# Closing an attention and FFN kernel by whole PSUM banks, with a new instruction order

## Chip, cores and metric

One NeuronCore of a Trainium2 chip runs the whole program. The metric is the device time of one execution in microseconds (us). Engines are named as in the profile: PE (TensorE), ACT (ScalarE), DVE (VectorE), POOL (GpSimd), SP (the DMA queue).

## What is computed

```python
xn  = layernorm(x)                       # x: 1 x 2048 x 640
q   = (xn @ wq) -> 32 heads of 20        # wq: 640 x 640
k, v = xn @ wk, xn @ wv                  # one key/value head of 20 for all heads
p   = softmax(q k^T / sqrt(20))          # 32 x 2048 x 2048
A   = concat(p v) @ wo                   # wo: 640 x 640
B   = silu(xn @ w1) @ w2                 # w1: 640 x 1728, w2: 1728 x 640
out = x + A + B                          # bfloat16
```

## The kernel before

**Tiles.** The 2048 query rows are cut into four chunks of 512 (`qc`), the heads into eight groups of four. A chunk and a head group form one of 32 groups (`g`), and each has 16 key tiles of 128. One score tile is 128 keys by 512 queries of one head: 2048 of them in all. With a head dimension of 20 padded to 32, the scores of up to four heads run at the same time in four row strips of the array (a burst, `s_mm`, L1168), and the product with the values runs as four column strips, one per head (a value step, `pv_mms`, L1295).

**Two ways to exponentiate.** ACT takes runs of one, two or three neighbouring PSUM banks with one exponential (L1258). DVE takes single tiles: it writes a 16-bit integer whose bits read as a bfloat16 power of two (`p1`, L1503), and adds two shifted copies of it (`SHIFT`), by integer additions over four tiles at once, so that three value steps together give the exponential. Four such tiles are a batch. The shifted copies are made on POOL (L1542) or DVE (L1547); each kind has two buffers (`NW`). In `dve_advance` copy 2 always goes to POOL (`POOL_J`), and copy 1 as the order's token says.

**The rest of PE's work.** Q projections, the FFN's first product with a tanh on ACT, and the FFN's second product joined with the output projection (`out_job`, two halves of 320 columns per 128 rows) are cut into pieces between the scores. All of them use `col_mm` (L537), four column strips per step. A finished group is copied out of PSUM (L1344), its sums are inverted, spread by small DMAs, multiplied on POOL (L950) and packed by DMAs into `oT`.

**The end.** For the last chunk the FFN's second product is made early (`y_job`: eight jobs of 320 columns, 14 contraction steps each; for row tiles 2 and 3 with the first three of the projection's 128-row steps, `YC = (0, 0, 3, 3)`) and gathered with half weight and the residual in `yx` (L1009). The last two groups are not packed: their sums are taken by PE against a selector `sel4` (L1089), inverted (L1092), spread by PE against an identity (L1107), and multiplied (L1116). Selector and identity are rebuilt late in the run on POOL (`make_sel`, from L1627) in a slot of `qT`. Then `fin_job` lays the chunk's 2560 output columns out as five banks of 512: `finA` does the projection steps that are left and the group before the last, `finB` the last group, and each bank is evicted with the addition of `yx` on DVE (L1057) and stored (L1074).

**Order.** `build` plans every engine's instruction order from estimated costs. From a planned 36 us on it instead follows written lists: `ORDER` has one three-character token for each PE step (S or s: scores for ACT, with the number of tiles; D, E, F, G: a score tile for DVE; a, d: value steps for ACT's and DVE's tiles; n, m: first and further steps of another job), and `OTHERS` has one letter for each instruction of ACT, DVE and POOL. Where the lists end, the planner goes on by its rules. `emit` then turns the order into instructions with semaphores; PE runs strictly in that order.

Of the kernel before, what the change touches and what calls it, by code (L numbers as in the profile page):

```python
# [14 lines left out]
P = 128  # L15
D = 640
# [65 lines left out]
POOL_J = (2,)  # L82
# [4 lines left out]
YC = (0, 0, 3, 3)  # L87
# [5 lines left out]
FIN_ACT = ()  # L93
FIN_ORDER = (1, 3, 0, 2, 4)
REST = 6
OUT_ACT = (1, 3)
T_SUM = 225.0
T_SPREAD = 230.0
AHEAD = 1
# [12 lines left out]
def rule(n):  # L112
# [4 lines left out]
    "D32D13S14a97nq6m00m00D25S20Dd2m00m00S23nh5aa7S20D66m00D32D03S14m00m00m00S20S12Dd6ab7nh4m00m00m00m00S20D33D05nh6m00m00m00m00nh2S20D23Dd4m00m00m00m00ac7"  # L117
    "S20S13D45nh6m00m00m00m00S30D34ad7ae7af7d03d13d33S24D26d23S20E37D82d43d63d53S24D16a03S20D37D82d93d73dc3S34E27a13D10S11D32d83df3nh7m00S24E20Dd6m00m00m00"
    "S21D00a23da3di3S34D20db3S21Dc7a33nh0m00m00S24E36D27m00m00nh1m00m00m00m00S34D12a43de3dd3a53dg3S20E37dh3S24Dd2D26a63nh7m00S20D02m00S14Dc5D56m00m00a73S20"
    "E32s24a83nq6m00m00m00m00S20D22E37dk3dj3S24a06d06S30d36d26a16S24D93D27d66d56S20D02d96d16d46S23D95a26nh7m00S20D32m00S23D25d86m00dc6m00S20D02S15db6nh3d76"  # L120
    "m00m00m00m00S20E34De7a36a46a56D02S24da6df6S20D33dd6E17S24nh2m00m00S20De3m00D07S24m00de6dh6S20D33De7a66dg6a76S24D12a86nh3m00S20D37m00D02S24a96m00S20Da7"
    "m00d02d32a02E14D05S26d22d42S20D33nq4m00m00S25D17m00m00S20Da3a12d62S25D07a22d52S20D34d12d92S25E13D87a32d82S20D24dc2da2S25D13Dc7a42nh4m00S20E33m00S25D17"
    "m00D23S20a52db2S25Dc3D57m00a62df2de2S20D33d72a72S25Dc7nh3m00m00m00m00S20D24a82dh2S26D55nh4m00m00D30D21S13m00m00S35nh3m00m00m00m00a92S20E34s25dd2dg2a07"
    "d07d17S20Da4D33d37S25D02a17d27d67S20Da4d47S25D12D03a27d57S20D34nh2m00m00m00m00S23E15D86s20a37d97d87d77dc7D13S24Dc2a47D26S20da7nh3m00S24D52a57E36D20S11"
    "m00m00m00S24E32a67db7S20Dd6df7de7S24D02nh3m00m00m00m00S20D26Dd2s24a77dh7dd7dg7S20D63a87nq6m00S24D32m00S20D93m00m00S24D02a97d03d33S20D66a03d23S24D32D07"
    "d43S20D96a13d63S24E32nh7m00D06D20S11m00m00m00S34E32a23a33d53d93S20Dd2d73D07S24D36dc3d83nh2S20E27m00Dc6S14D25m00m00m00S20D16S17nh4m00m00m00m00db3S20D35"
    "de3a43d13S35De2a53S20D04a63nh2m00m00m00S34D37a73da3a83dd3S10E11m00S24De6D37a93nh0m00S16S11m00m00S24Da2F06S17m00aa3d01d31S24E12d21d11d61S26D03d41d51S24"
    "D10Da2a01d91S26D33nh0m00D04D15S12m00m00m00S26E33a11a21d81S24D82dc1S26D20db1dd1df1S22D14S15a31nh0m00m00m00m00de1S22D34s25Dd7a41d71da1nq4m00S22D00m00D27"
# [12 lines left out]
    "S20D15E27de2dd2S23D86a82a92D15S20no7m00S23D36m00m00m00m00aa2S20S25m00m00m00d04d14d34d24D20S11S12D93m00a04d64d54D00S11S15D36d94m00m00d84S22S10E21m00m00"
    "m00m00d44S25Dc1m00m00m00a14S22D20d74S25D11Dc7a24a34S22E30nh1m00m00m00m00S25D10s22D27a44a54da4dc4db4S20Dc5D56df4dd4S22E37de4nh5m00S20Dc6a64D27S12E33m00"
    "m00m00S20D36a74S22D17dg4dh4nh6m00S20D85a84D22D13S17m00m00m00S30S15nh7m00m00m00m00a94d03S30D36d33d23d63d53d93S24D27d83d13S20D82a03a13S24D16D27a23a33S20"
    "E32d43d73nh6S24Dd7m00m00m00m00S20D02s24D27a43a53dc3da3df3S20E36Dc2db3dg3S24D17nh6m00m00D20S11E32m00m00S24Dc7a63a73dd3S20D22de3S24D16a83nh7m00S20E32m00"
    "D86D14S15a93m00m00dh3S30D26nh5m00m00m00m00S23D87s20D32a06d06d36d26d66S33D17a16nh2m00m00m00m00d56S20s33D27a26d96d86d16d46D30D81S12d76nh7m00D13S24D20m00"
    "m00m00E31Dc2S13s24a36a46dc6S20D23da6df6db6S24D12Dc7a56S20E33dd6nh2m00S24D17a66m00m00m00S20D23E37nh4m00m00m00m00a76S20S12Dd5de6nh3m00m00m00m00S20D04S17"
    "nq2m00m00m00m00S24S10D31a86a96dg6dh6S22S24F21D87nq0m00m00m00m00S21D13a06d06S24D37d16d36S20E22D93a16d26S24D07d46d66S20D22D93a26d56S24E37d76d96a36S30D23"
    "d86S24D07dc6db6nq3m00m00S20D32m00m00S24Dc7a46a56da6S20D22dd6S24D13Dc7a66df6de6S20E32D23dg6S24a76D12s20E37Fc3dh6S24D12a86D27S20G33s24a96d02S20Da7d32d62"
    "D03S24D16a02d22S20D37no3m00m00m00S24D86d52d92S20D27m00m00m00m00d82S24S26m00m00m00m00m00m00d12S20D14D85a12m00m00m00m00S26E34m00a22S20D15a32a42S23D27E36"
    "d42d72dc2S20Dc5a52S23D27D36da2db2no5m00S20m00m00S23De6m00m00m00m00S20E17m00m00m00S23D36m00m00m00m00S20D07m00m00m00m00S23Da6a62a72a82S20D15D07a92df2S23"  # L150
    "D36de2dd2S20E15D87dg2S23D26dh2no5m00m00m00S20D17m00m00m00S32m00m00m00m00S20D96D67m00m00m00m00m00m00S32D46m00m00a07d07d17S20D36d37d27S22Dc4D55a17a27d67"
    "S20E36d47d57S22Dc4a37S25D20E31a47d87d77S22D14nq0m00S25D21m00m00m00S23Dc2a57d97S25E30D21dc7da7S22D14db7no0m00S25E31m00m00S23Dc2m00a67a77a87S21S25m00m00"
    "m00m00m00m00m00m00S21D23D34m00m00m00a97de7S25E13dd7S21Da4m00m00m00S25D03aa7d04d34d24S30D33a04S25D17d64d54d14nq3d44S30D87m00m00m00m00S25a14S20D17Dc2a24"
    "a34d94d84S25D23E37dc4db4S20D12d74no3m00S25D27m00m00S20Dc2m00m00m00a44m00S35D32m00m00m00m00m00da4S20D12m00m00S25D37m00m00m00m00a54S20E27D92a64a74S25D03"
    "a84dd4S30D27de4S25D83a94df4dh4dg4S20D37D22no3m00m00m00m00S24D16m00m00m00m00S20E37m00m00m00S34D92m00m00m00S20D07m00m00m00m00a02S34D27d02d12d32d22S20Dc3"
    "D57a12a22a32d42S24E33D26d62d52S20Dc7a42S23E35no6m00a52S20D17m00m00m00m00d92S33D37m00m00m00d72d82S20D27m00m00Dc3S14D25m00m00da2S20D17m00m00dc2S23E35db2"
    "S20Dc7m00m00m00m00a62S23D25D37a72a82S20E16de2dd2S33Db7a92aa2no6m00S20D17m00m00S32D05m00m00m00m00d07S20D25m00d17d37d27S22S14D95m00m00m00m00m00m00m00m00"
    "m00S30D03m00a07d67d47S23D25d97d57S20Dc2D56a17d87S24E33dc7d77S20Dc2a27a37S23D25E36nh2a47m00S20D15m00S23D26a57da7m00db7S25Dc0D51m00nh3m00m00m00m00S24D30"
    "S16a67nh1m00m00m00m00S32D25dd7df7a77de7S25D80a87dh7S11D32S13D24a97nh0m00dg7S25D11D82m00m00m00S23E37s25a01a11d01d11d21S22D24D30d31d41S26E15a21d61S22Da4"
# [259 lines left out]
def build(nc, A_x, A_wq, A_wk, A_wv, A_wo, B_x, B_w1, B_w2, out, stack):  # L419
# [584 lines left out]
    def y_job(qc, i, hf):  # L1004
# [8 lines left out]
        job.consumers = [op]  # L1013
        return job

    oT_op = {}
    fin_made = {}
    fin_asked = set()

# [1373 lines left out]
```

## Time and profile before

| | |
|---|---|
| runs | 681.31, 680.39, 681.21 us; median 681.21 |
| profiled execution | 681.22 us; its span, first to last instruction, 679.4 us |
| granted TensorE clock, mean | 0.995 |
| DVE's score tiles / shifts on DVE / shifts on POOL | 712 / 118 / 238 |
| exponentials of one, two, three banks | 56 / 520 / 80 |

The profile has one row for each group of instructions of one source line, engine and operation: how often, the busy time, the mean of one, and the idle time ahead of them. Busy shares are averages over the whole span; the windows cut it into stretches. In the last of 40 equal slices PE is 80% busy, DVE 30%, ACT 20% and POOL not at all.

### The profile page before, as it was taken

The numbers are of one execution on the slowest core, as the hardware profiler recorded it, in microseconds if no ns is written. First come the engines' busy times: TensorE is split into PE (matmuls) and PEld (weight loads), VectorE is DVE, ScalarE is ACT, GpSimd is POOL, SyncE is SP. The second block draws the span as 40 slices with busy tenths as digits, with TensorE's granted clock in tenths as the row PEclk, the third lists the DMA queues.
The fourth block names the chain that finished last, engine by engine and source line by source line (L and its number), as shares of the span: only waits on it lengthen the run. The fifth ranks groups of instructions, "written<-read, shape, count | busy, mean of one in ns | idle before, by whom it ended". The sixth has DMA issues, their size and how long they took to land.

```text
span 679.4 us, 22817 instructions
## 1 busy us (share of the span) xinstructions
PE 666.0 (98%) x9898; PEld 240.8 (35%) x9901; DVE 632.2 (93%) x1102; ACT 654.4 (96%) x728; POOL 514.1 (76%) x314
## 2 busy tenths in 40 slices
PE   8999999999999999999999999999999999999998
PEld 5433323332322333333333333333332333333345
DVE  7899999999998999899999999999999899999943
ACT  6999999999998999999999999999999899999992
POOL 6648787878886887876888787788888857777760
PEclk9999999999998999999999999999999899999999
DMA  8652220222221223231212222312222202233201
GB/s 224 184 180 18 32 24 14 27 26 22 34 32 24 32 30 42 29 57 25 23 27 35 36 26 34 40 31 50 21 19 35 25 20 33 31 49 43 23 7 41
DMA packets 34243, 29.00 MB, mean 43 GB/s; under 512 B 15486, under 2 KB 29662, under 8 KB 34142
## 3 DMA queue, kind: packets, MB, share of 16 engines
q1 hardware_dynamic: 33854, 27.20, 25.9%
q8 instruction: 78, 1.28, 0.8%
q10 hardware_dynamic: 288, 0.33, 0.1%
q14 instruction: 23, 0.19, 0.1%
HBM read 11.09 MB, written 2.62 MB: 20 GB/s over the span
## 4 chain that ended last, share of the span: by engine, by line
PE 63%; ACT 20%; DVE 13%; POOL 3%; issue 1%; DMA 0%; POOLq 0%; ACTq 0%
PE psall L1295 21%; PE psall L1168 20%; PE psall L537 20%; ACT sbt L1258 18%; DVE sbt L1503 7%; POOL sbt L1542 3%; ACT sbt L863 1%; DVE sbt L1547 1%; DVE sbt L866 1%; DVE sbt L653 1%; DVE sbt L697 0%; DVE sbt L655 0%; PE psall L711 0%; DVE sbt L783 0%; DVE sbt L1344 0%
## 5 line engine op out<-in xcount | busy, mean ns | idle before, releaser
L1258 ACT ACTIVATE sbt<-psall 128x1024 bf16<-128x1024 f32 (+2 forms) x656 | 624.4, 1067 | 7.1 <-PE psall L1168 5.7
L1542 POOL TENSOR_SCALAR sbt<-sbt 128x2048 int16<-128x2048 int16 x238 | 451.5, 1897 | 112.3 <-PE psall L1295 40.9
L1503 DVE TENSOR_SCALAR sbt<-psall 128x512 int16<-128x512 f32 x712 | 454.6, 682 | 20.3 <-PE psall L1168 15.2
L1295 PE MATMUL psall<-sbt 128*32 128x512 bf16 x3472 | 273.6, 386 | 2.1 <-DVE sbt L1547 0.8
L1168 PE MATMUL psall<-sbt 32*128 32x512 bf16 x2048 | 255.8, 386 | 4.4 <-ACT sbt L1258 1.0
L537 PE MATMUL psall<-sbt 128*32 128x320 bf16 (+3 forms) x3900 | 218.9, 332 | 0.4 <-DVE sbt L1503 0.2
L1168 PEld LDWEIGHTS psall<-sbt 32*128 32x128 bf16 x2048 | 69.3, 91 | 225.6 <-ACT sbt L1258 125.6
L537 PEld LDWEIGHTS psall<-sbt 128*32 128x32 bf16 (+1 forms) x3900 | 84.2, 96 | 86.8 <-issue 46.6
L1295 PEld LDWEIGHTS psall<-sbt 128*32 128x32 bf16 x3472 | 72.8, 95 | 109.2 <-issue 70.6
L1547 DVE TENSOR_SCALAR sbt<-sbt 128x2048 int16<-128x2048 int16 x118 | 80.8, 710 | 0.6 <-PE psall L1295 0.5
L950 POOL TENSOR_TENSOR sbt<-sbt 128x512 bf16<-128x512 f32 x30 | 38.5, 1284 | 20.2 <-DVE sbt L1547 16.8
L866 DVE SCALAR_TENSOR_TENSOR sbt<-sbt,psall 128x512 bf16<-128x512 bf16 x52 | 35.1, 677 | 0.1
L863 ACT ACTIVATE sbt<-psall 128x512 bf16<-128x512 f32 x52 | 32.1, 619 | 0.0
L1344 DVE COPY sbt<-psall 128x512 f32<-128x512 f32 x31 | 21.1, 681 | 0.4 <-PE psall L1295 0.3
L783 DVE TENSOR_SCALAR sbt<-psall 128x512 bf16<-128x512 f32 x20 | 13.6, 678 | 0.1
L1009 DVE SCALAR_TENSOR_TENSOR sbt<-psall,sbt 128x320 f32<-128x320 f32 x8 | 3.9, 486 | 10.2 <-PE psall L537 10.2
L662 POOL TENSOR_TENSOR sbt<-sbt 128x2 f32<-128x2 f32 x8 | 5.7, 708 | 8.5 <-DVE sbt L660 8.2
L993 DVE SCALAR_TENSOR_TENSOR sbt<-psall,sbt 128x320 bf16<-128x320 f32 x24 | 11.6, 485 | 0.2 <-PE psall L537 0.2
L675 POOL TENSOR_SCALAR sbt<-sbt 128x640 bf16<-128x640 bf16 x12 | 10.4, 874 | 1.5 <-DVE sbt L667 1.5
L653 DVE BATCH_NORM_STATS2 sbt<-sbt 128x6 f32<-128x320 bf16 x14 | 6.6, 472 | 1.9 <-DMA sbt<-in_A_x_dram 1.9
L685 PE MATMUL psall<-sbt 128*128 128x128 bf16 x80 | 6.9, 220 | 1.5 <-DVE sbt L678 1.5
L1824 PE MATMUL psall<-sbt 128*32 128x256 bf16 x144 | 6.5, 338 | 1.2 <-DVE sbt L577 1.2
(63 smaller groups left out, 98.8 us busy)
## 6 DMA issues: line engine op xcount, KB each, us to landing
sbt<-sbt SPq DMA_DIRECT2D x120, 64.0 KB, 3.8
sbt<-in_A_x_dram SPq DMA_DIRECT2D x28, 160.0 KB, 4.1
sbt<-sbt SPq DMA_DIRECT2D x213, 20.0 KB
out_dram<-sbt SPq DMA_DIRECT2D x14, 160.0 KB, 2.1
sbt<-in_B_w_dram SPq DMA_DIRECT2D x1, 2160.0 KB, 13.9
sbt<-in_B_w_dram SPq DMA_DIRECT2D x1, 2080.0 KB, 8.4
sbt<-sbt SPq DMA_DIRECT2D x75, 8.0 KB
sbt<-in_A_wq_dram SPq DMA_DIRECT2D x1, 800.0 KB, 5.8
```

What stands on the lines that cost most here:

```text
L537: ins = pe.matmul(ps[j * SLOT:(j + 1) * SLOT, b * BANK + off:b * BANK + off + n], w[:, j * SLOT:(j + 1) * SLOT], x, start=start, stop=stop ...
L783: op = Op("dve", lambda v: v.tensor_scalar_mul(q_st[:, st, :], bk(job.bank), QSCALE), t_dve(512), DVE_END, pre=[job.ready], writes=[res("q ...
L863: t = Op("act", lambda a: a.activation(t_buf[0:rows, ts, :], bk(job.bank, 0, QW, rows=rows), AF.Tanh, scale=0.5), t_act(512), ACT_END, pre ...
L866: u = Op("dve", lambda v: v.scalar_tensor_tensor(out=hT[par][0:rows, fk, :], in0=t_buf[0:rows, ts, :], scalar=1.0, in1=bk(job.bank, 0, QW, ...
L950: nm = pool(lambda e: e.tensor_tensor(oU[:, us, :], U_sb[:, us, :], Rrep, ALU.mult), 1356.0, POOL_END, pre=[uc] + lc + pack_op.get(divmod( ...
L1168: return pe.matmul(bk(b), kT_rep[i * SLOT:(i + 1) * SLOT, kt * P:(kt + 1) * P], qT[i * SLOT:(i + 1) * SLOT, g % NQ, :], start=True, stop=T ...
L1258: return a.activation(Ebuf[:, es * QW:es * QW + w], ps[:, buf[0] * BANK:buf[0] * BANK + w], AF.Exp, scale=ESCALE)
L1295: ins = pe.matmul(ps[i * SLOT:(i + 1) * SLOT, ub * BANK:ub * BANK + QW], lhsT, rhs, start=(first and k < HG), stop=(last and k >= len(lst) ...
L1344: return v.tensor_copy(U_sb[:, us, :], bk(ub))
L1503: p1 = Op("dve", lambda v: v.tensor_scalar(z16[:, i * QW:(i + 1) * QW], bk(job.bank), ZBIAS, 0.0, ALU.add, ALU.max), t_dve(QW) + 2.0, DVE_ ...
L1542: op = pool(lambda v, t=t, j=j, zin=zin: v.tensor_scalar(t.bitcast(I16), zin, float(SHIFT[j]), 1.0, ALU.add, ALU.mult), POOL_SHIFT, POOL_E ...
L1547: op = dve(lambda v, t=t, j=j, zin=zin: v.tensor_scalar_add(t.bitcast(I16), zin, float(SHIFT[j])), t_dve(N, 4), prio=SPRIO - 0.01 * j, **args)
```

## The change

- `y_job` is made per bank: five jobs of 512 columns with 14 steps, none of the projection (`YC` all zero). A bank that spans two row tiles is filled by two matmul groups per step. The sum is gathered in SBUF (`yxf`).
- A new `w_job` per bank adds the projection's first three steps (`WC = 3`) into the same SBUF sum with one more DVE operation. `y` and `w` jobs are both named in `ORDER`.
- `fin_job` is left with the projection's fourth step and the group before the last (one piece of two steps per bank); the first such piece is named in `ORDER`, too. The closing steps run in the bank order 1, 0, 2, 3, 4.
- Bank 0 is evicted by ACT into `U_sb` and added on POOL; the other four stay on DVE.
- The fp32 identity keeps an SBUF tile of its own; the selector is a strided view of it. `make_sel` and `make_two` are gone.
- A new token `J` puts both shifted copies on DVE; the packing DMAs have an earlier rank.
- `ORDER` and `OTHERS` are new from beginning to end and reach the last value step.

Counted in the lists (those before, then after): score bursts for ACT of one, two, three tiles 56/496/69, then 88/504/62; score tiles for DVE 705, then 716; value steps 831, then 863; shifts on DVE 116, then 110; shifts on POOL 234, then 250; bursts of scores, which hold ACT's and DVE's tiles together, 601, then 605.

```diff
-POOL_J = (2,)
-YC = (0, 0, 3, 3)
+YC = (0, 0, 0, 0, 0)
+WC = 3
-FIN_ACT = ()
-FIN_ORDER = (1, 3, 0, 2, 4)
+FIN_ACT = (0,)
+FIN_ORDER = (0, 1, 2, 3, 4)
+FIN_B = (1, 0, 2, 3, 4)
...
-    ident_f = s_t[-1][-1][:, 0:2 * P].bitcast(F32)
+    ident_f = sb([P, P], F32)
-    sel4 = qT[:, 2, 0:2 * HG].bitcast(F32)
-    ident_e = qT[:, 2, QW - 2 * P:QW].bitcast(F32)
...
+    def bank_mms(b, lhs, rhs, pre, reads, rows=tuple(range(HG))):
+        op = Op("pe", None, sum(t_mc(d1 - d0) for _, d0, d1, _ in segs(b)), pre=pre, reads=reads, mode="p")
+        def f(pe, bank):
+            sg = segs(b)
+            for i, d0, d1, off in sg:
+                ins = col_mm(pe, bank, d1 - d0, lhs(i), rhs(i, d0, d1), op.ends[0] and off == 0, op.ends[1] and i == sg[-1][0], off)
+            return ins
...
+    def y_job(b):
+        job = bank_job(f"y{b}", ffn_bank(b) + o_bank(b, range(YC[b])))
+        op = Op("dve", lambda v: v.scalar_tensor_tensor(out=yxf[:, b * BANK:(b + 1) * BANK], in0=bk(job.bank), scalar=0.5,
+                                                        in1=xresf[:, b * BANK:(b + 1) * BANK], op0=ALU.mult, op1=ALU.add),
...
+    def w_job(b):
+        job = bank_job(f"w{b}", o_bank(b, range(YC[b], WC)))
+        op = Op("dve", lambda v: v.scalar_tensor_tensor(out=yxf[:, b * BANK:(b + 1) * BANK], in0=bk(job.bank), scalar=0.5,
+                                                        in1=yxf[:, b * BANK:(b + 1) * BANK], op0=ALU.mult, op1=ALU.add),
...
     def fin_job(b):
+        mms += o_bank(b, range(WC, DC - 1))
+        mms.append(bank_mms(b, lambda i: oT[:, 1 - qc % 2, 1, i * P:(i + 1) * P], lambda i, d0, d1: wo_end[:, 0, d0:d1],
+                            d_wo_end, [res("oT", "end", 1, 0)]))
...
+        if b in FIN_ACT:
+            half = U_sb[:, us, :]
+            op = Op("act", lambda a: a.activation(half, bk(job.bank), AF.Copy, scale=0.5), t_act(BANK), ACT_END, pre=args["pre"], writes=[res("U", us)], prio=0.3, job=job)
+            fin_ev[b] = pool(lambda g: g.tensor_tensor(dst, half, yb, ALU.add), 1356.0, POOL_END, pre=[op], reads=[res("U", us), res("yx", b)],
+                             writes=args["writes"], prio=0.3, on_commit=args["on_commit"])
...
-                return pe.matmul(bk(b, t * HG, (t + 1) * HG), U_sb[:, us, t * P:(t + 1) * P], sel4, start=True, stop=True)
+                return pe.matmul(bk(b, t * HG, (t + 1) * HG), U_sb[:, us, t * P:(t + 1) * P], ident_f[:, DH:P:SLOT], start=True, stop=True)
...
-            if j in POOL_J or st.get("pool", pool_load() < ru.pj):
+            if j > st.get("pool", 0 if pool_load() < ru.pj else 1):
...
-    "d94d84ny2m00m00S25E37m00S20Dc3m00da4d74dc4S35D33m00m00m00m00a54S10E21m00a64S35D33m00m00m00m00db4S20D13m00m00m00S25D87a74a84S30E23a94df4S35")
+    "S16a84d94d74d84a94S30J35aa4dc4da4db4S35S13dd4de4ny0m00m00m00m00S35D21m00m00m00m00S21S13D94m00m00m00m00S34D07m00a01a11a21S22D37a31d01S34D90a41d31d11d41"
+    "S22D07D30d51d21d61S34E27a51S22D00d71ns7m00m00m00S34D30a61a71S22E27np0m00m00m00S24S26d91d81nw2m00a81da1S33dc1m00a91db1dd1de1nf6m00aa1")
```

More of the change, by code (lines that the diff above doesn't have):

```diff
@@ L1002, in build @@
     y_op = {}
-    def y_job(qc, i, hf):
-        e0, e1 = hf * HALF, (hf + 1) * HALF
-        mms = ffn_mms(qc, i, e0, e1, True, not YC[i]) + o_mms(qc, i, e0, e1, False, True, range(YC[i]))
-        job = pe_job(f"y{qc}_{i}_{hf}", mms, (14 + YC[i]) * 140, dyn=True)
-        short(job, qc)
-        op = Op("dve", lambda v: v.scalar_tensor_tensor(out=yx[:, i, e0:e1], in0=bk(job.bank, 0, HALF), scalar=0.5,
-                                                        in1=xres[:, i, e0:e1], op0=ALU.mult, op1=ALU.add),
-                t_dve(HALF), DVE_END, pre=[job.ready, xres_op[(qc, i)]] + [norm_op[n] for n in range(NT)] + [out_done[(qc - 1, t)] for t in range(QTP)], reads=[res("xres", i)], writes=[res("yx", i, hf)], prio=0.3, job=job)
-        y_op[(i, hf)] = op
[L1013 to L1018, printed above, removed]
     def segs(b):
@@ new lines, in bank_job, with xr_of @@
+    def bank_job(name, mms):
+        job = Job(name, 1100)
+        for k, op in enumerate(mms):
+            op.job, op.name, op.first, op.last = job, name, k == 0, k == len(mms) - 1
+            op.ends = (k == 0, k == len(mms) - 1)
+        job.mms.extend(mms)
+        job.ops = list(mms)
+        job.ready = mms[-1]
+        job.gate = None
+        return job
+    def xr_of(b):
+        return [xres_op[(QC - 1, i)] for i, *_ in segs(b)], [res("xres", i) for i, *_ in segs(b)]
+    def y_job(b):
+        qc = QC - 1
+        job = bank_job(f"y{b}", ffn_bank(b) + o_bank(b, range(YC[b])))
+        pre, rd = xr_of(b)
+        op = Op("dve", lambda v: v.scalar_tensor_tensor(out=yxf[:, b * BANK:(b + 1) * BANK], in0=bk(job.bank), scalar=0.5,
+                                                        in1=xresf[:, b * BANK:(b + 1) * BANK], op0=ALU.mult, op1=ALU.add),
+                t_dve(BANK), DVE_END, pre=[job.ready] + pre + [norm_op[n] for n in range(NT)] + [out_done[(qc - 1, t)] for t in range(QTP)],
+                reads=rd, writes=[res("yx", b)], prio=0.3, job=job)
+        y_op[b] = op
+        job.consumers = [op]
+        return job
@@ L1029, in fin_job @@
+    oT_op = {}
+    fin_made = {}
     def fin_job(b):
         qc = QC - 1
[L1031 to L1033 removed]
         mms = []
[L1035 to L1041 removed]
@@ L1042, in fin_job @@
-        for i, d0, d1, off in segs(b):
-            fresh = not mms
-            rest = o_mms(qc, i, d0, d1, fresh, False, range(YC[i], DC - 1), off)
-            mms += rest
-            def fa(pe, bank, i=i, d0=d0, d1=d1, off=off, first=not mms):
-                return col_mm(pe, bank, d1 - d0, oT[:, 1 - qc % 2, 1, i * P:(i + 1) * P], wo_end[:, 0, d0:d1], first, False, off)
-            mms.append((fa, t_mc(d1 - d0), "p", [oT_op[(1, 0)]] + d_wo_end, [res("oT", "end", 1, 0)]))
-        job = pe_job(f"fin{b}", mms, len(mms) * 140)
+        mms += o_bank(b, range(WC, DC - 1))
@@ L1672, in fin_a @@
     def fin_a(b):
-        job = fin_job(b)
-        at = misc_front.index(("finA", b))
-        for k in range(len(job.ops) - 1, 0, -1):
-            misc_front.insert(at + 1, Piece(job, job.ops[k:k + 1]))
-        return Piece(job, job.ops[:1])
+        return Piece(fin_job(b))
     def fin_b(b):
@@ L2137, in follow @@
                     return None
-                q[i] = Piece(MAKE[a](*q[i][1:]))
+                got = MAKE[a](*q[i][1:])
+                q[i] = got if isinstance(got, Piece) else Piece(got)
                 q[i].kind = a
             m = q[i]
-            if not open_(m) or b not in sc.free:
-                return None
-            m.job.want = b
+            if m.job.bank is None:
+                if not open_(m) or b not in sc.free:
+                    return None
+                m.job.want = b
             op, what = m.mms[0], ("new", (m, src))
@@ L2149, in follow @@
             return None
-        if k == "n" or k in "DE" or k in "ad" and fresh_u():
+        if k == "n" and m.job.bank is None or k in "DEJ" or k in "ad" and fresh_u():
             e = max(e, bank_at(b, op.mode))
```

284 lines of the change are left out of this document (138 added, 146 removed).

## The prediction

> **What bounds the kernel now.** I read the page, then the windows by stage, the groups by shape, the waits, and last the timeline of the final 25 us. The page first:
>
> ```profile
> span 679.4 us, 22817 instructions
> PE 666.0 (98%) x9898; PEld 240.8 (35%) x9901; DVE 632.2 (93%) x1102; ACT 654.4 (96%) x728; POOL 514.1 (76%) x314
> ```
>
> Four engines are nearly full, so shares alone decide nothing. The windows (busy us of PE, PEld, DVE, ACT, POOL in each stretch) separate the stages:
>
> ```profile
> 36.00:600.00 564.00, 558.35 (x8068) 189.30 (x8064) 545.43 (x913) 558.76 (x629) 445.89 (x246) 0.99 0.24 33
> 640.00:660.00 20.00, 20.00 (x335) 8.48 (x331) 13.04 (x22) 19.98 (x19) 15.39 (x9) 1.00 0.20 19
> 660.00:667.00 7.00, 7.00 (x158) 3.59 (x154) 0.84 (x2) 6.80 (x6) 0.00 (x0) 1.00 0.02 5
> 667.00:672.00 5.00, 5.00 (x143) 4.10 (x136) 1.90 (x6) 0.66 (x2) 0.00 (x0) 1.00 0.02 3
> 672.00:680.00 8.00, 4.08 (x112) 2.64 (x104) 3.39 (x5) 0.00 (x0) 0.00 (x0) 1.00 0.24 84
> ```
>
> Two stages with different limits show. Up to 667 us the exponentials on ACT run almost without a gap (558.76 of 564, then 19.98 of 20), while from 640 on DVE lies idle for 20 - 13.04 + 7 - 0.84 = 13.1 us: its share of the scores is used up before ACT's. Behind 667 ACT is empty and a serial drain of 12.4 us follows, most of it PE. The waits (us, times, longest, from 36 to 660 for ACT, over the span for the others) say how hard the coupling is:
>
> ```profile
> ACT sbt L1258 <- PE psall L1168: 4.1, 5, 1.7
> PEld psall L1168 <- ACT sbt L1258: 125.6, 352, 1.2
> PEld psall L1295 <- POOL sbt L1542: 7.9, 26, 0.7
> POOL sbt L1542 <- DVE sbt L1547: 29.7, 27, 1.8
> ```
>
> ACT waited 4.1 us for scores; the weight loads of the scores waited 125.6 us for ACT to free a bank. So ACT is the clock of the long stage, and PE follows with reserve. I therefore cost three things: ACT's list, PE's list ahead of the last exponential, and the drain.
>
> **ACT's list.** The groups by shape (busy, mean ns):
>
> ```profile
> L1258 ACT ACTIVATE sbt<-psall 128x1024 bf16<-128x1024 f32 x520 | 494.9, 1049 | 6.6 <-PE psall L1168 5.7
> L1258 ACT ACTIVATE sbt<-psall 128x1536 bf16<-128x1536 f32 x80 | 116.1, 1485 | 0.2
> L1258 ACT ACTIVATE sbt<-psall 128x512 bf16<-128x512 f32 x56 | 34.8, 632 | 0.3
> L1503 DVE TENSOR_SCALAR sbt<-psall 128x512 int16<-128x512 f32 x712 | 454.6, 682 | 20.3 <-PE psall L1168 15.2
> L1547 DVE TENSOR_SCALAR sbt<-sbt 128x2048 int16<-128x2048 int16 x118 | 80.8, 710 | 0.6 <-PE psall L1295 0.5
> L1542 POOL TENSOR_SCALAR sbt<-sbt 128x2048 int16<-128x2048 int16 x238 | 451.5, 1897 | 112.3 <-PE psall L1295 40.9 <-DVE sbt L1547 29.7 <-PE psall L537 10.5
> ```
>
> There are 2048 score tiles: 712 go to DVE, so 520 x 2 + 80 x 3 + 56 = 1336 to ACT. The new lists name 110 shifts on DVE and 250 on GpSimd, 360 in all, two for each batch of four: 180 batches, 720 tiles on DVE, 1328 on ACT. The old score tokens cover 56 + 496 x 2 + 69 x 3 = 1255 of ACT's tiles and leave 81; the new ones cover 88 + 504 x 2 + 62 x 3 = 1282 and leave 46, which I take as 23 pairs ahead of the list, as the prologue is unchanged (the other 35 of before follow its list). After: 88 singles, 527 pairs, 62 triples. Successive exponentials overlap; the timeline has nine triples in 12.29 us:
>
> ```profile
> 654.51 12.29 ACT L1258 ACTIVATE sbt<-psall 128x1536 bf16<-128x1536 f32 x9
> ```
>
> So (9 x 1.485 - 12.29) / 8 = 0.134 us of each lie under the next, and a single costs 0.498, a pair 0.915, a triple 1.351. Before: 27.9 + 475.8 + 108.1 = 611.8. After: 43.8 + 482.2 + 83.8 = 609.8. The eight tiles fewer are worth 3.4 us; 21 more instructions give 1.4 back. Net -2.0 us. DVE takes eight tiles more (8 x 0.682 = 5.5) and eight shifts fewer (8 x 0.710 = 5.7): nothing, and the 13.1 us idle at the end are there for the five gathering evictions.
>
> **PE's list ahead of the last exponential.** What a step costs is read where the stage is dense:
>
> ```profile
> 657.46 0.39 PE L1168 MATMUL psall<-sbt 32*128 32x512 bf16 x3
> 657.78 0.83 PE L1295 MATMUL psall<-sbt 128*32 128x512 bf16 x12
> 658.44 0.45 PE L537 MATMUL psall<-sbt 128*32 128x320 bf16 x8
> 658.82 0.39 PE L1168 MATMUL psall<-sbt 32*128 32x512 bf16 x3
> ```
>
> Three steps of four column tiles take 0.66 (657.78 to 658.44), so 0.22 each; a burst of scores with its two turns takes about 0.42 (0.32 to the next kind, 0.1 back). Counting the tokens, the old list has 601 bursts and needs at least 12 more for the 35 tiles behind it; the new one has 605: -8 x 0.42 = -3.4. Two more DVE batches add four value steps: +0.9. The last job of the old FFN (x56 below, 2.07) and the projection's twelve steps of tiles 0 and 1 (about 1.6), which now follow the last exponential, move ahead of it, with the first bank's two-step tail (0.44): about +4.0. In sum +1.5 us. What hides it is the reserve in the 125.6 us of waits; if that reserve is missing late in the stage, the last value step comes 1.5 us later instead of 2.0 earlier. I take it as hidden, because the added DVE batches and the earlier end of ACT's list leave the final 27 us less lopsided than the 13.1 idle us of DVE show now.
>
> The identity kept in SBUF and the packing DMAs' earlier rank touch these rows:
>
> ```profile
> PE psall L1168 <- POOL sbt L1627: 0.7, 1, 0.7
> L950 POOL TENSOR_TENSOR sbt<-sbt 128x512 bf16<-128x512 f32 x30 | 38.5, 1284 | 20.2 <-DVE sbt L1547 16.8 <-DMA sbt<-sbt 2.3
> ```
>
> The first is the only wait for the old rebuilt identity, once 0.7 us of PE, which the reserve hides; it goes. The rank moves issues on SP's queue ahead of the chunk loads and stores, with the ring transfers of the next group behind them; the engine that would feel it is GpSimd at its normalising multiply, which waited 2.3 us for transfers in the whole run. Both at nothing; without cover 0.7 better or 2.3 worse.
>
> **The drain.** Its rows:
>
> ```profile
> 666.85 0.40 PE L1295 MATMUL psall<-sbt 128*32 128x512 bf16 x4
> 667.08 2.07 PE L537 MATMUL psall<-sbt 128*32 128x320 bf16 x56
> 667.30 0.66 ACT L1396 ACTIVATE sbt<-psall 128x256 f32<-128x256 f32 x2 [0.51 <-PE psall L1295]
> 669.08 1.05 PE L1089 MATMUL psall<-sbt 128*128 128x4 f32 x8
> 670.07 1.08 PE L1107 MATMUL psall<-sbt 128*32 128x128 f32 x32
> 670.78 0.86 DVE L1116 TENSOR_TENSOR sbt<-sbt,psall 128x256 bf16<-128x256 f32 x2 [0.40 <-PE psall L1107]
> 670.97 5.11 PE L537 MATMUL psall<-sbt 128*32 128x128 bf16 x144
> 675.47 1.34 DVE L1057 SCALAR_TENSOR_TENSOR sbt<-psall,sbt 128x512 bf16<-128x512 f32 x2 [0.30 <-PE psall L537]
> ```
>
> I count from the last value step at 666.85. Its copies end at 1.11; but PE is still in the last FFN job, so the sums start at 2.23; the multiplies end at 4.79; then come all 36 projection steps of all five banks (x144), though only eight of them need the multiplies; the last eviction ends at 9.96 and the span 2.6 later, at 12.6. After the change, four two-step pieces (chunk 3 and the group before the last, 0.44 each) and the closing step of each bank are left. One piece can delay the sums: start at 1.2. From the sums' start to the end of the multiplies is 2.56 before (669.08 to 671.64), and I add 0.4 for a piece in between: 4.2. The five closing steps (1.1) run under the evictions, the first of which starts at about 4.4. Four on VectorE take 3 x 0.66 + 0.69 = 2.7: 7.1. With the 2.6 of the store the drain is 9.7: -2.9. Bounds: all four pieces ahead of the sums 10.9 (-1.7); none in the way 8.7 (-3.9).
>
> The fifth bank goes ACT copy, then GpSimd add. Beside L950 above, the nearest row for a two-input 128x512 operation is VectorE's eviction:
>
> ```profile
> L1057 DVE SCALAR_TENSOR_TENSOR sbt<-psall,sbt 128x512 bf16<-128x512 f32 x5 | 3.4, 691 | 1.8 <-PE psall L537 1.8
> ```
>
> Copy 0.63 (as a single exponential) and add 1.28, with 0.2 for the handovers (an estimate: 0.05 lies between the last exponential's end at 666.80 and the value step that waits for it, and I take twice that for each), make 2.1 from the second closing step, 0.6 less than the four evictions beside it; a fifth one on VectorE would add 0.66. [...]
>
> **Sum.** 681.22 (the profiled execution, 1.8 beyond its span; the median of the runs is 681.21) - 2.0 - 2.9 = 676.3.
>
> **Rivals.** (a) GpSimd becomes the bound, and the kernel slower. It gets 12 shifts more, 12 x 1.897 = 22.8 on 514.1. Against it: 118 us unused between 36 and 600. For it: 26 value steps already waited 7.9 us for its shifts, and each kind of shift has two buffers, so a late one stops PE's queue, and ACT behind it. It decides from the point where over a fifth of the 22.8 (4.9) falls into stretches in which GpSimd has no gap; at a third, 7.6: 683.9. (b) The moved PE work is not hidden: +1.5 in place of -2.0: 679.8, about even with the measurable bound. (c) The drain is not shortened, because the pieces queue ahead of the sums and the evictions wait as now: 679.2. [...] (e) The flatter order also removes ACT's 4.1 us of waits: 672.3.
>
> **How the numbers follow.** Forecast 0.53; (a) 0.12; (b) 0.12; (c) 0.08; (d) 0.08; (e) 0.07. A difference under 0.2% (1.4 us) can't be told from none. Faster: the forecast, (c), (d), (e) and half of (b), 0.82; same 0.06; slower 0.12. The forecast's own range is 675.3 to 677.5 by the drain's bounds, and a us or two of list waits either way; down to 672.3 for (e) and up to 680.5 for (b) leaves about 0.15 out.
>
> **What would show it.** After: ACT 88/527/62 exponentials without wider gaps, the last one ending near 664.8; the sums about 1.2 after the last value step instead of 2.2; no x144 block behind the multiplies; under 10 us from the last value step to the end. Wrong: waits of value steps on GpSimd well over 7.9, ACT waiting on scores for over 6 us, or a GpSimd add that ends behind the last VectorE eviction.

## The result and the profile after

Before 680.80 us (median of 4 runs, 678.86 to 681.31), after 671.44 us (median of 4 runs, 671.05 to 671.78): ratio 0.9868, 95% interval 0.9846 to 0.9889. The kernel became 9.4 us faster, where the prediction had 4.9 and a lower end of 672.3. The direction was right, the size was not. The profiled execution of after took 671.75 us, its span is 669.9 us; against the profiled one of before (681.22) that is -9.5 us, and this is the difference taken apart here. Lines have moved: exponentials L1301, scores L1211, value steps L1336, `col_mm` L536, evictions L1100, ACT's copy L1096, POOL's addition L1097.

The page of after:

```profile
span 669.9 us, 22826 instructions
PE 660.0 (99%) x9919; PEld 240.1 (36%) x9919; DVE 632.8 (94%) x1103; ACT 652.7 (97%) x750; POOL 535.5 (80%) x322
```

The groups by shape of after show the lists as they were counted: 88, 527 and 62 exponentials, 720 tiles on DVE, 250 and 110 shifts.

```profile
L1301 ACT ACTIVATE sbt<-psall 128x1024 bf16<-128x1024 f32 x527 | 501.5, 1060 | 3.1 <-PE psall L1211 2.5
L1572 POOL TENSOR_SCALAR sbt<-sbt 128x2048 int16<-128x2048 int16 x250 | 474.3, 1897 | 94.3 <-DVE sbt L1577 25.1 <-PE psall L1211 19.4 <-PE psall L1336 19.2
L1533 DVE TENSOR_SCALAR sbt<-psall 128x512 int16<-128x512 f32 x720 | 458.1, 681 | 21.0 <-PE psall L1211 16.4
...
L1301 ACT ACTIVATE sbt<-psall 128x1536 bf16<-128x1536 f32 x62 | 91.4, 1478 | 0.4 <-PE psall L1211 0.2
...
L1577 DVE TENSOR_SCALAR sbt<-sbt 128x2048 int16<-128x2048 int16 x110 | 74.6, 710 | 0.2
...
L1301 ACT ACTIVATE sbt<-psall 128x512 bf16<-128x512 f32 x88 | 53.9, 626 | 0.2
```

So the surprise is not in what is executed. The timeline of the end of after:

```profile
661.08 0.40 PE L1336 MATMUL psall<-sbt 128*32 128x512 bf16 x4
...
661.31 0.61 PE L536 MATMUL psall<-sbt 96*32 96x128 bf16 x16
661.53 0.66 ACT L1434 ACTIVATE sbt<-psall 128x256 f32<-128x256 f32 x2 [0.50 <-PE psall L1336]
...
661.97 1.05 PE L1132 MATMUL psall<-sbt 128*128 128x4 f32 x8
...
662.96 1.08 PE L1150 MATMUL psall<-sbt 128*32 128x128 f32 x32
...
663.67 0.86 DVE L1159 TENSOR_TENSOR sbt<-sbt,psall 128x256 bf16<-128x256 f32 x2 [0.40 <-PE psall L1150]
...
663.85 2.59 PE L536 MATMUL psall<-sbt 96*32 96x256 bf16 x72
664.74 2.48 DVE L1100 SCALAR_TENSOR_TENSOR sbt<-psall,sbt 128x512 bf16<-128x512 f32 x4 [0.21 <-PE psall L536]
664.95 0.60 ACT L1096 ACTIVATE sbt<-psall 128x512 f32<-128x512 f32 x1 [2.76 <-PE psall L536]
665.63 1.27 POOL L1097 TENSOR_TENSOR sbt<-sbt 128x512 bf16<-128x512 f32 x1 [5.84 <-ACT sbt L1096]
```

The last value step starts at 661.08 instead of 666.85, 5.8 us earlier; the drain behind it lasts to 669.9, 8.8 us instead of 12.6. So 3.7 us come from the drain (2.9 predicted) and 5.8 from the list ahead of it (2.0 predicted). The larger miss is the list's.

The windows divide the list's part. The columns are the stretch, its length, busy us and instructions of PE, PEld, DVE, ACT and POOL, granted clock, DMA share and GB/s; each list of windows ends 0.4 us behind the last value step. The rows are the two stretches in which ACT's idle time changes most, and the sum from 30 us on, first of before, then of after:

```profile
210.00:510.00 300.00, 299.37 (x4524) 104.01 (x4520) 288.17 (x483) 297.30 (x334) 240.91 (x132) 1.00 0.25 32
510.00:570.00 60.00, 58.29 (x844) 19.69 (x840) 56.34 (x95) 57.83 (x61) 46.00 (x28) 0.97 0.24 28
...
sum 637.25, PE 630.86 PEld 218.67 DVE 602.00 ACT 630.64 POOL 494.65; mean PE 105.14 PEld 36.44 DVE 100.33 ACT 105.11 POOL 82.44
```

```profile
210.00:510.00 300.00, 298.94 (x4534) 103.95 (x4530) 292.39 (x490) 299.32 (x334) 251.36 (x139) 1.00 0.26 33
510.00:570.00 60.00, 60.00 (x921) 21.40 (x917) 58.97 (x99) 60.00 (x68) 50.27 (x28) 1.00 0.23 26
...
sum 631.50, PE 627.95 PEld 220.58 DVE 604.07 ACT 628.34 POOL 514.78; mean PE 104.66 PEld 36.76 DVE 100.68 ACT 104.72 POOL 85.80
```

ACT's busy time falls from 630.64 to 628.34, by 2.3: the -2.0 of the prediction. ACT's idle time falls from 637.25 - 630.64 = 6.6 to 631.50 - 628.34 = 3.2, by 3.4: the prediction left it as it was. And the row 510 to 570 of before has a mark beside its 2.2 idle us of ACT: a granted clock of 0.97. Finer windows of before show what that is, there and at the start of the stretch ahead of it:

```profile
199.20:202.60 3.40, 3.30 (x36) 0.95 (x34) 3.40 (x6) 3.40 (x4) 2.10 (x2) 1.00 0.39 27
202.60:206.00 3.40, 2.91 (x27) 0.79 (x23) 3.40 (x7) 3.40 (x5) 3.00 (x2) 1.00 0.69 75
206.00:209.40 3.40, 2.23 (x21) 0.60 (x21) 3.40 (x5) 3.40 (x4) 1.56 (x1) 1.00 0.12 28
209.40:212.80 3.40, 3.31 (x28) 0.70 (x28) 2.63 (x6) 1.66 (x2) 2.53 (x2) 0.50 0.10 24
...
523.40:526.80 3.40, 3.06 (x30) 0.95 (x28) 3.38 (x7) 3.40 (x4) 3.24 (x3) 1.00 0.21 36
526.80:530.20 3.40, 2.40 (x24) 0.62 (x23) 3.40 (x6) 3.40 (x4) 3.19 (x3) 1.00 0.10 25
530.20:533.60 3.40, 3.32 (x34) 1.04 (x34) 1.68 (x4) 1.60 (x3) 3.08 (x4) 0.51 0.07 14
```

In two places the old order has run out of other jobs, and PE has only scores and value steps. Ahead of the half clock these wait for DVE more than for ACT: from 199.2 to 209.4 us the weight loads of the scores waited 2.5 us for DVE's exponentials and 1.1 us for ACT's, from 520 to 530.2 us 2.1 and 1.6. PE's matmuls thin out (36, 27, 21 and 30, 24 in 3.4 us each), and then the clock is half for 3.4 us. In that time ACT is busy only 1.66 and 1.60 us: starved by PE, 1.7 to 1.8 us lost each time. These two places also hold all five of the waits that make up ACT's 4.1 us between 36 and 660 us: 2.0 us between 209 and 217, 2.0 us between 526 and 538, none elsewhere. In after a thin stretch near the first of these places has 37, 37, 27 and 38 matmuls in 3.4 us each, at full clock:

```profile
196.50:199.90 3.40, 3.35 (x37) 0.92 (x33) 3.40 (x7) 3.40 (x5) 2.69 (x2) 1.00 0.28 28
199.90:203.30 3.40, 3.10 (x37) 0.97 (x34) 3.37 (x6) 3.40 (x5) 3.24 (x3) 1.00 0.83 70
203.30:206.70 3.40, 3.14 (x27) 0.90 (x24) 3.32 (x6) 3.40 (x5) 2.63 (x2) 1.00 0.11 24
206.70:210.10 3.40, 3.19 (x38) 0.79 (x35) 3.40 (x7) 3.40 (x4) 2.51 (x2) 1.00 0.00 0
```

The theory for the list's part: two half-clock stretches, each following on a lean stretch of PE, and ACT's shorter list. The rivals: only the list and the new order's fewer waits (then idle work for PE changes nothing), or the clock is a symptom (then ACT waits the same at full clock).

### The profile page after: what moved, and what is told of

Its sections match the earlier page's. It is cut to its first block, busy times and chain, and to the rows that moved or that the text cites. A ratio compares the mean times of both kernels' runs of the same rounds, so it can differ in the third digit from the quotient of the medians.

```text
span 669.9 us, 22826 instructions
## 1 busy us (share of the span) xinstructions
PE 660.0 (99%) x9919; PEld 240.1 (36%) x9919; DVE 632.8 (94%) x1103; ACT 652.7 (97%) x750; POOL 535.5 (80%) x322
## 3 DMA queue, kind: packets, MB, share of 16 engines
q8 instruction: 78, 1.28, 0.8%
## 4 chain that ended last, share of the span: by engine, by line
PE 79%; ACT 10%; DVE 8%; POOL 1%; issue 0%; DMA 0%; DVEq 0%; POOLq 0%; ACTq 0%
PE psall L1336 28%; PE psall L1211 25%; PE psall L536 24%; ACT sbt L1301 9%; DVE sbt L1533 5%; DVE sbt L1577 1%; POOL sbt L1572 1%; PE psall L710 1%; PE psall L684 1%; DVE sbt L782 0%; DVE sbt L1385 0%; DMA sbt<-in_A_x_dram 0%; PE psall L1150 0%; PE psall L1132 0%; DVE sbt L1100 0%
## 5 line engine op out<-in xcount | busy, mean ns | idle before, releaser
L1301 ACT ACTIVATE sbt<-psall 128x1024 bf16<-128x1024 f32 (+2 forms) x677 | 622.7, 1042 | 3.7 <-PE psall L1211 2.7
L1572 POOL TENSOR_SCALAR sbt<-sbt 128x2048 int16<-128x2048 int16 x250 | 474.3, 1897 | 94.3 <-DVE sbt L1577 25.1
L1336 PE MATMUL psall<-sbt 128*32 128x512 bf16 x3488 | 274.4, 384 | 0.8 <-POOL sbt L1572 0.2
L1211 PE MATMUL psall<-sbt 32*128 32x512 bf16 x2048 | 251.1, 384 | 2.8 <-ACT sbt L1301 1.1
L536 PE MATMUL psall<-sbt 128*32 128x512 bf16 (+4 forms) x3904 | 216.9, 331 | 0.1
L1211 PEld LDWEIGHTS psall<-sbt 32*128 32x128 bf16 x2048 | 69.1, 91 | 222.0 <-ACT sbt L1301 137.3
L536 PEld LDWEIGHTS psall<-sbt 128*32 128x32 bf16 x3904 | 84.5, 95 | 82.6 <-issue 40.2
L1336 PEld LDWEIGHTS psall<-sbt 128*32 128x32 bf16 x3488 | 71.0, 94 | 108.3 <-issue 73.9
L1577 DVE TENSOR_SCALAR sbt<-sbt 128x2048 int16<-128x2048 int16 x110 | 74.6, 710 | 0.2
L992 DVE SCALAR_TENSOR_TENSOR sbt<-psall,sbt 128x320 bf16<-128x320 f32 x24 | 11.6, 485 | 0.6 <-PE psall L536 0.6
L674 POOL TENSOR_SCALAR sbt<-sbt 128x640 bf16<-128x640 bf16 x12 | 10.4, 874 | 1.5 <-DVE sbt L666 1.5
L696 DVE COPY sbt<-psall 128x640 bf16<-128x640 bf16 x14 | 6.4, 482 | 1.0 <-PE psall L684 1.0
```

The costliest lines, as they stand in the source:

```text
L536: ins = pe.matmul(ps[j * SLOT:(j + 1) * SLOT, b * BANK + off:b * BANK + off + n], w[:, j * SLOT:(j + 1) * SLOT], x, start=start, stop=stop ...
L1211: return pe.matmul(bk(b), kT_rep[i * SLOT:(i + 1) * SLOT, kt * P:(kt + 1) * P], qT[i * SLOT:(i + 1) * SLOT, g % NQ, :], start=True, stop=T ...
L1301: return a.activation(Ebuf[:, es * QW:es * QW + w], ps[:, buf[0] * BANK:buf[0] * BANK + w], AF.Exp, scale=ESCALE)
L1336: ins = pe.matmul(ps[i * SLOT:(i + 1) * SLOT, ub * BANK:ub * BANK + QW], lhsT, rhs, start=(first and k < HG), stop=(last and k >= len(lst) ...
L1572: op = pool(lambda v, t=t, j=j, zin=zin: v.tensor_scalar(t.bitcast(I16), zin, float(SHIFT[j]), 1.0, ALU.add, ALU.mult), POOL_SHIFT, POOL_E ...
L1577: op = dve(lambda v, t=t, j=j, zin=zin: v.tensor_scalar_add(t.bitcast(I16), zin, float(SHIFT[j])), t_dve(N, 4), prio=SPRIO - 0.01 * j, **args)
```

## The experiments

Each is compared with the kernel before on the same chip, 4 to 11 executions against 7 to 21 of before. Ratios are to before; the two numbers behind a ratio are its 95% interval.

**1 and 2. The kernel before with idle PE work in the lean stretches.** A new token `x` makes one value step without effect on any result:

```diff
+        elif k == "x":
+            op, what = filler(999.0), ("fill", None)
```

It stands 19 times in the first run, between other value steps of both stretches, and 10 times in the second, in the first stretch only.

> The kernel before with 19 idle value steps (zeros times zeros, added to the open group's bank) put into its order, 10 between 197 and 209 us and 9 between 518 and 530 us, where the trace of before has no job for PE but scores and value steps and the granted clock then halves for 3.4 us. Theory A (PE streams too little there, the clock halves, and ACT loses about 2.1 us each time): both half-clock stretches go, clock 1.000, 676.5 to 677.5, about 4.0 less than before. Rival B (the half clock is incidental, or is made up elsewhere): no change within 0.7 us. Rival C (PE has no reserve there): 19 x 0.22 = 4.2 us slower.

> The same with the 10 idle value steps between 197 and 209 us alone. Theory A: one half-clock stretch is left, near 528 us, clock 0.997 to 0.998, about 2.0 us less than before. Rival B: no change within 0.7 us. Rival C: 2.2 us slower.

Measured: 679.48 us against 680.03 (ratio 0.999, 0.9981 to 0.9999), and 679.61 (0.9996, 0.9987 to 1.0005). With both stretches filled the profiled execution kept the full clock throughout, and 10 of the 11 executions had a mean clock of at least 0.999. With one filled, the profiled execution still had its half clock in the other, at 528, and 5 of the 11 had a mean of 0.997 or less. Of the 21 executions of before beside them 20 had 0.997 or less. But so many steps stand in ACT's way: in the filled stretch of the first run ACT is busy 3.28, 3.17 and 3.14 of 3.40 us where the kernel before had 3.40:

```profile
195.80:199.20 3.40, 3.40 (x46) 1.08 (x47) 3.19 (x6) 3.28 (x5) 3.24 (x3) 1.00 0.10 24
199.20:202.60 3.40, 3.40 (x46) 0.95 (x38) 3.40 (x6) 3.17 (x4) 1.61 (x2) 1.00 0.39 27
202.60:206.00 3.40, 3.19 (x35) 0.84 (x34) 3.04 (x6) 3.14 (x4) 3.32 (x2) 1.00 0.73 76
```

So the half clock could be bought off here with idle work, but 19 steps at 0.22 us seem to give most of it back. These two runs show that the clock follows PE's work. They do not show what the half clock costs.

**3. Only nine idle steps, where PE stood still.** The kernel before with `x` at the places where its PE was idle for about a step (six between 203 and 209.5 us, three between 523 and 528).

> The kernel before with only 9 idle value steps, each where PE stood idle for 0.2 us or more in the trace of before (six between 203 and 209.5 us, three between 523 and 528), so that they delay no scores. Theory A2 (a half-clock stretch is worth about 2 us, and the 19 steps of b_fill2 gave part of it back by delaying scores): clock 1.000, ACT's gaps near 209 and 530 gone without new ones, 2.0 to 4.0 us less than runs that have both stretches. Rival B2 (what the stretch costs is made up anyway, the value steps there wait for shifts whatever the clock): no more than the 0.6 us of b_fill2.

Measured: 678.46 us (11 runs, 678.35 to 679.16) against 679.58 (17 runs, 679.14 to 681.58), ratio 0.9979 (0.9971 to 0.9988). This kernel executes the same exponentials and the same drain as before, and is faster by doing more. All 11 executions had a clock of at least 0.999. The profiled execution has a span of 676.8 us and its last value step at 664.29. Two of its short windows, the sum from 30 us to 0.4 behind the last value step, and that step in the timeline:

```profile
206.00:209.40 3.40, 3.12 (x42) 1.04 (x41) 3.40 (x5) 3.40 (x4) 1.74 (x1) 1.00 0.11 25
209.40:212.80 3.40, 3.40 (x58) 1.10 (x50) 3.40 (x7) 2.66 (x4) 2.29 (x2) 1.00 0.10 25
```

```profile
sum 634.70, PE 630.54 PEld 219.13 DVE 602.71 ACT 630.80 POOL 495.16; mean PE 105.09 PEld 36.52 DVE 100.45 ACT 105.13 POOL 82.53
```

```profile
664.29 0.40 PE L1296 MATMUL psall<-sbt 128*32 128x512 bf16 x4
```

ACT's busy time is that of before (630.80 to 630.64), its idle time 634.70 - 630.80 = 3.9 instead of 6.6, and the last value step comes 666.85 - 664.29 = 2.6 us earlier. So the two half-clock stretches were 2.6 us of the profiled execution of before. Of ACT's 4.1 us of waits 1.2 are left, in the same two places.

How many such stretches an execution has varies. One of 3.4 us at half clock takes 0.5 x 3.4 / 678 = 0.0025 off the mean clock, so a mean of 0.997 fits one and 0.995 two, as in the profiled executions of run 2 and of before. On this run's chip 13 executions of the unchanged kernel had 0.997, with a median of 679.44 us, and two had 0.995, at 680.72 and 681.25: 1.0 and 2.3 to 2.8 us more than the 678.46 here. Single executions scatter too much to show it. On one chip the unchanged kernel took 678.71 us at a clock of 1.0, below the 679.67 to 680.22 beside it at 0.995 to 0.997; on another 679.28 at 1.0, no less than the fastest beside it at 0.997 (679.23). Between the medians, with the mix of executions as it came, the stretches are worth 1.1 us. The rival that the clock is a symptom falls; the one that lists and waits are all falls too, for these 2.6 us.

**4 and 5. The new program under the old lists.** All of the change but the lists: `ORDER` and `OTHERS` of before, less three tokens that the shorter job no longer has; the second run also has the idle steps.

> The new program (bank jobs, kept identity, split last eviction) under the old order lists; only the three last steps of the old list's fifth FFN job, which no longer exist, are taken out. Theory A (the new order, not the new jobs, is worth the larger part): both half-clock stretches stay, clock 0.995; the drain gets 1 to 3 us shorter, and the wider FFN steps cost PE some us late in the stage: 678 to 681. Rival D (the new jobs are worth it all): 671 to 674.

> The kernel h_old with the 19 idle value steps. Theory A: about 4 us less than h_old, clock 1.000. Rival B: as h_old. If what is left to the kernel after is then about 2 to 4 us, that is ACT's shorter list and the list's last part.

Measured: 682.40 us (ratio 1.0036, 1.0022 to 1.005) and 682.87 (1.004, 1.0026 to 1.0054): slower than before. The end of the first run:

```profile
671.49 0.40 PE L1334 MATMUL psall<-sbt 128*32 128x512 bf16 x4
...
675.24 2.48 DVE L1098 SCALAR_TENSOR_TENSOR sbt<-psall,sbt 128x512 bf16<-128x512 f32 x4 [0.21 <-PE psall L534]
```

And the window 570 to 660 of the same run, then of before:

```profile
570.00:660.00 90.00, 89.49 (x1540) 35.33 (x1541) 80.16 (x132) 85.59 (x85) 63.13 (x36) 1.00 0.23 30
```

```profile
570.00:660.00 90.00, 89.97 (x1482) 34.67 (x1474) 80.15 (x133) 89.58 (x90) 67.90 (x39) 1.00 0.23 31
```

The drain is that of after (680.4 - 671.49 = 8.9), but the last value step comes 4.6 us later than before. Between 570 and 660 ACT is busy 85.59 of 90 us, where before had 89.58: the moved jobs make ACT wait there, as rival (b) of the prediction had it. Under the new lists the same program ends its value steps at 661.08, 10.4 us earlier. So the drain's gain exists only together with an order that has room for what was moved. The idle steps of the second run kept the clock at 0.999 and gained nothing, where about 4 us had been expected. Behind 570 ACT is as idle as without them; between 30 and 570 its idle time fell only from 4.6 to 4.3 us. The half clock went, but as in run 1 the 19 steps make ACT wait themselves (0.5 us between 150 and 210, where it had not waited).

**6. All five evictions on DVE.**

```diff
-FIN_ACT = (0,)
+FIN_ACT = ()
```

> The kernel after with all five last evictions on VectorE (the ACT copy and the GpSimd add taken out). By the trace of after (four evictions in 2.48 us, the GpSimd add ending 0.3 us ahead of the last one): a fifth in the row adds 0.6 us, 672.0 to 672.1. [...]

Measured: 671.92 us (ratio 0.9876, 0.9857 to 0.9895), which cannot be told from after. The profiled execution's drain is 670.8 - 661.70 = 9.1, 0.3 longer than after's. The evictions now last 3.08 instead of 2.48, the 0.6 of the prediction, but the span ends 2.4 behind them instead of 2.7. The prediction's rows wanted the addition split off (2.1 us from the second closing step, 0.6 less than the evictions beside it); 671.92 us here and 671.44 us of after show no difference that can be measured.

```profile
661.70 0.40 PE L1336 MATMUL psall<-sbt 128*32 128x512 bf16 x4
...
665.36 3.08 DVE L1100 SCALAR_TENSOR_TENSOR sbt<-psall,sbt 128x512 bf16<-128x512 f32 x5 [0.21 <-PE psall L536]
```

This kernel has the same order as after, and two of its four runs took 671.19 and 671.26 us at a granted clock of 0.999 or more, the other two 672.57 and 672.85 at 0.996. The windows of the profiled one show where:

```profile
182.60:186.00 3.40, 3.10 (x33) 0.94 (x29) 3.30 (x6) 3.40 (x5) 3.24 (x3) 1.00 0.46 25
186.00:189.40 3.40, 2.99 (x29) 0.70 (x30) 3.40 (x6) 3.40 (x4) 1.53 (x1) 0.80 0.64 78
189.40:192.80 3.40, 3.40 (x42) 1.05 (x39) 2.02 (x5) 2.03 (x3) 1.90 (x2) 0.70 0.09 19
```

The new order still has a lean place: the profiled execution had its half clock there, and the two executions at 0.996 took 1.3 to 1.7 us longer than the other two.

**7. The three projection chunks left at the end.** `WC = 0`, and the tokens and letters of the `w` jobs taken out.

> The kernel after with the projection's first three steps taken out of the gathered jobs and put back into the closing pieces of each bank (no w jobs; their tokens and letters taken out of the lists). If moving them ahead of the last value step shortened the drain: the 12 steps of the four last pieces, 12 x 0.22 = 2.6 us more behind it, and 0 to 1.0 us less ahead of it: 673.0 to 674.0. Rival (the drain's length is set by the chain of copies, sums and evictions, and PE has room beside it): 671 to 671.8.

Measured: 675.20 us (ratio 0.9924, 0.9906 to 0.9941). The drain is 673.6 - 662.01 = 11.6, 2.8 longer than after's:

```profile
662.01 0.40 PE L1336 MATMUL psall<-sbt 128*32 128x512 bf16 x4
...
664.88 5.64 PE L536 MATMUL psall<-sbt 128*32 128x128 bf16 x172
666.42 0.69 DVE L1100 SCALAR_TENSOR_TENSOR sbt<-psall,sbt 128x512 bf16<-128x512 f32 x1 [0.87 <-PE psall L536]
...
667.95 0.69 DVE L1100 SCALAR_TENSOR_TENSOR sbt<-psall,sbt 128x512 bf16<-128x512 f32 x1 [0.84 <-PE psall L536]
```

The long block behind the multiplies is back, and each eviction waits for its bank again (1.3 to 1.5 apart instead of 0.6). So three quarters of the drain's 3.7 us are these chunks. The total rises by 3.8 us, more than the drain and more than was expected. The last value step comes 0.9 later in the profiled execution, whose clock was 0.997: it fell into the lean place of run 6 (ACT busy 2.02 of 3.40 us from 189.4 to 192.8). Two runs at 1.0 took 673.57 and 673.60 us, 2.1 to 2.2 more than after.

**8. Triples cut up.** The new order with each of its 62 triples as a pair and a single: the same tiles on ACT in 62 more exponentials.

> The kernel after with each of its 62 three-bank exponentials cut into one of two banks and one of one; the scores are unchanged. If ACT's list sets the end of the long stage: 62 more instructions of 0.06 us each (0.498 + 0.915 - 1.351), 3.3 to 3.9 us more: 675. If PE, DVE or GpSimd sets it and ACT has reserve: 0 to 1 us more.

Measured: 673.76 us (ratio 0.9905, 0.9891 to 0.9919), 2.3 us more than after. By the prediction's figures (0.915 + 0.498 - 1.351) x 62 = 3.8 us were to be added to ACT's list. The trace shows less: from 30 us on ACT is busy 631.00 us where after had 628.34, so 2.7 us for 62 more exponentials, 0.043 each.

```profile
662.82 0.40 PE L1339 MATMUL psall<-sbt 128*32 128x512 bf16 x4
```

The last value step comes 662.82 - 661.08 = 1.7 us later in the profiled execution. About two thirds of the added time reached the end; the rest went into ACT's idle time, which became 0.9 us shorter. So ACT's list is the bound of the long stage for most of the time, not for all of it.

**9 and 10. After with idle steps, and with two swaps.** Eight `x` tokens between 183 and 206 us; in the second run also one burst of scores moved ahead of one step, at 606.6 and at 659.0 us. By the trace of after ACT has its longest wait at the first, 0.50 us, and none at the second.

> The kernel after, with eight idle value steps (about 1.8 us of PE in all) where its own PE stood still between 183 and 206 us and had little but scores and value steps; they compute nothing. Theory (a half-clock stretch costs 1 to 1.5 us and comes in some executions only): no half-clock stretch in any execution, the fast executions of after unchanged, so a median of 671.0 to 671.4 with less scatter, ratio to the kernel before 0.986 to 0.988. Rival (PE's list sets the time, every idle step counts): 671.4 + 1.8 = 673.2.

> The same with two swaps in the order, where ACT waited 0.5 and 0.66 us for scores behind other steps of PE: one burst of three tiles at 659.0 us ahead of one value step, one burst at 606.6 ahead of one step of the FFN job. If ACT's list sets the end there, each swap is worth at most one step, 0.2 us, together 0.3 to 0.4: 670.7 to 671.1. If the waits come back at the next burst, as the idle steps' small waits did in the kernel before, no change against the run without the swaps.

Measured: 671.65 us (0.988, 0.9863 to 0.9896) and 671.91 us (0.9885, 0.987 to 0.99). Neither is better than after. The four runs of the first lie within 0.15 us at clocks of 0.999 to 1.0, but the four of after had these clocks as well, so that the idle steps protect the lean place is not shown. The medians differ by 0.2 us where 1.8 us of PE time were added, so where PE stood still, the idle work was nearly free. The swaps gained nothing: ACT's single wait of 0.50 us at 607 became two, of 0.28 and 0.45 us, at the bursts around the swap. So no version beat the changed kernel.

## Why the prediction was wrong

**The count of the list: right.** 88, 527 and 62 exponentials, DVE's 720 and POOL's 250 are those predicted; ACT's busy time fell by 2.3 us (2.0 predicted). The price of one more exponential was too high: run 8 has 0.043 us, where the sum took about 0.065 (1.4 us for 21).

**ACT's waits: the step that failed.** "ACT is the clock of the long stage, and PE follows with reserve", and so the 4.1 us in which ACT waited were left unchanged in the sum, with 0.07 for rival (e), which removes them (by 676.3 - 4.1 its time is 672.2, not 672.3). By the waits they fell to 1.1 us:

```profile
ACT sbt L1301 <- PE psall L1211: 1.1, 3, 0.5
```

Together with gaps too short to be listed as waits, ACT's idle time fell by 3.4 us, and 2.6 of these were the half clock (run 3). Rival (e) comes nearest to what happened, but it names a flatter order and no clock.

The clue stood in the prediction's own rows. The longest of only five waits was 1.7 us, and the row 36 to 600 had a granted clock of 0.99 beside 1.00 in all the others. A mean below 0.995 over 564 us is, at the half clock of the two windows (0.50 and 0.51), at the least 0.005 x 564 x 2 = 5.6 us; asking where they lay would have found both stretches, and all of ACT's 4.1 us at them. PE's waiting was read as harmless reserve. In the two lean places it was not: there it bunched (2.23 and 2.40 busy of 3.40 us), more of it was for DVE (2.5 and 2.1 us) than for ACT (1.1 and 1.6), and the work that ACT then waited for ran at a clock of 0.50 and 0.51.

**PE's list, +1.5 taken as hidden: right under the new order only.** Run 4 shows the same work not hidden: the last value step 4.6 us later under the old one, where rival (b) had put the price at 1.5.

**The drain: right in mechanism, short by 0.8.** Sized at 9.7, measured 8.8. The sums started 0.9 behind the last value step, not 1.2: at 661.97 they are under way before the two copies end at 662.19, and the piece ahead of them fits in; and no piece stood between the sums and the multiplies (663.67 + 0.86 - 661.97 = 2.56, exactly as before), where 0.4 had been added. The evictions ran in 2.48 (2.7). It is the end "none in the way" of the bounds, 8.7.

**The split eviction.** The copy and the addition took 0.60 and 1.27 us (0.63 and 1.28 assumed), and the addition ended 0.3 before the last one on DVE, so (d), an addition that ends last, did not come; but run 6 shows that the path it spares is worth 0.3 us in the profile, too little to measure.

**GpSimd as the bound (a): no.** 250 shifts at the same 1897 ns, and 94.3 us idle are left ahead of them (112.3 before).

**The sum, remade for the profiled executions.** Drain -3.7; half clock -2.6 (run 3); from run 3's last value step (664.29) to after's (661.08) -3.2, of it ACT's busy list 630.80 - 628.34 = -2.5 and its other waits 3.9 - 3.2 = -0.7. Together -9.5. By the same stretches as above those 0.7 us are two things: ACT's idle time from 210 to 570 us falls by 1.5 more (1.34 and 0.81 us in run 3, 0.68 and 0 in after), which takes in the 1.2 us of waits that run 3 had left at the two places, and from 570 to 630 us it rises by 0.7 (0.29 to 1.01). Which tokens of the order do this was not tested. Between medians the half-clock part is smaller, 1.1 us in run 3, as the executions of before differ in it. The later medians of the unchanged kernel were 679.58 to 680.03 us, not 680.80, so about 1 us of the 9.4 comes from which of its executions were compared; against those medians, too, the kernel gained over 8 us, not 4.9.

## What to carry to other kernels

Before an engine's reserve is called harmless, look where it lies: ask for the granted clock by short windows, and look for the place and the cause of any mean below 1.00; here 0.995 stood for two stretches of 3.4 us at half clock. Here the lean stretches of PE could be filled with steps that do nothing: nine in the gaps gained 1.1 us between medians, 19 among the other steps 0.55. Work taken off the drain is gained only if the order has room for it elsewhere: the same program was 2.4 us slower than before under the old order, and 9.4 faster under the new.

## What was not expected of the hardware

In the trace of before the clock is halved although PE looks busy. In the two windows ahead of the half clock at 209.4 the rows give 2.91 and 2.23 busy of 3.40 us, ahead of the one at 530.2 3.06 and 2.40; what was low is the number of matmuls, 27 and 21, 30 and 24. Four of these matmuls run at once in strips (a group of four takes 0.40 us, each of its matmuls 0.38), so the busy time of PE says little of how much streams. The half clock lasted 3.40 us each time, at 0.50 and 0.51, and no window ahead of it was idle: the leanest was 66% busy. The same order had it in some executions only (run 6: two of four at a mean of 0.996, two at 0.999 and 1.0). What exactly brings it on, and how many lean windows it takes, was not measured. A single lean window did not halve the clock: after has one of 27 matmuls between windows of 37 and 38, and before itself one of 26, 2.98 of 3.40 us busy, from 185.7 to 189.1 us, both at full clock.
